# A stored instruction order, searched again: the query weights' second transpose goes behind the tile transposes

## Chip, cores and metric

The kernel runs on one core of a Trainium2 chip. The metric is the device time of one execution in microseconds, the median of several runs. The profile is of one more execution of the same program.

## What is computed

One transformer block on x, 2048 rows of 448, in bf16: attention with a feature map in place of the softmax over keys, then a gated feed-forward part, each with a residual and a normalisation without weights ahead of it.

```python
h  = x + A(layernorm(x));  h2 = h + B(layernorm(h))
# A: 16 heads of 28
phi(t) = concat(softmax(t @ w_phi), softmax(-t @ w_phi))
kv = phi(k)^T v;  z = sum_s phi(k)
A = (phi(q) kv / (phi(q) z + 1e-6)) @ wo
# B: 448 -> 1792 -> 448
B = (sigmoid(y @ w_gate) * (y @ w_up)) @ w_down
```

## The kernel before

The 2048 rows are 16 tiles of 128. `build` does not emit instructions; it declares 884 tasks in a graph: a name, an engine (or two to choose from), a few instructions, what it depends on, and the PSUM banks it may take. `_Graph.stored` (L134) then reads a table of numbers, `ORDER` (L40). Each number is 32 times the task's index, plus four times the choice of banks, plus the choice of engine. Each engine executes its tasks in the order of the table, strictly one after another; `emit` (L255) adds the semaphore waits. SyncE's queue (SP) issues nearly all DMAs, in that order too. `TURNS` (L90) adds waits that the data do not need: the first task of each entry also waits for the second, to keep GpSimd (POOL) and VectorE (DVE) apart. `_Graph.order` (L155), which once made such tables from assumed durations, is not used while `ORDER` is filled.

The tasks in this text, with the lines under which the profile shows them:

- Loads at L468: `x` t (from tile t on), `wk`, `wv`, `wq` (raw key, value and query weights), `wph`, `wom` (eight pieces of the output weights), later `wg`, `wu`, `wd`.
- Fold of the key weights with w_phi: `kT` (TensorE transpose, L547), `WkT` (copy, L432), `wM` 1 (L562), `W2` 1 (copy, L432) into `Wk2`. `warm`, `fill` (L539, L995) are matmuls on zeros that keep TensorE (PE) busy; `kv0` (L710) opens bank 4.
- Fold of the query weights: `wqT` 0 and 1, two DMA transposes of `wq_raw` into `WqT` (L508, on SP); `wM` 0 (L562) needs both; `W2` 0 copies into `Wq2`.
- Tiles of x: `bst`, `agg`, `ve`, `rstd` (statistics; L590 to L596), `xn` (normalise, L609 or L610), then `xP`, `xT` (TensorE and a copy, L620 and L432) for tiles 0 to 3, and a DMA transpose `xT` 4, 6, ... 14 for two tiles each (L628, on SP).
- Keys and values (L644): pairs of 14 matmuls in two tasks, `pa` t and `pb` t (Wk2 and Wv of tile t; `va` 0, `vb` 0: Wv of tiles 0 and 1; `pa` 0, `pb` 0: Wk2 of both). A second half waits for its own first half. Then `ekp`, `ekm` (exponentials, ScalarE), `v1` (copy), `ss`, `rs`, `phi` (L685, L689, L691) and `kv` (L703), which sums over all tiles in bank 4; `kvz` (L758) takes it out.
- Queries (L743): `qa`, `q`, then `eqp`, `eqm` (L753).
- Output of pairs of tiles: `num` (L779), `ocp` (copy to `opm`, L432), `rSm`, `rr`, `b`, `c`, `rd`, `o`, `od` (VectorE, L795 to L826), `oT` (DMA transpose, L828; for pair 0 `oP` on TensorE, L815), `wr`, `woa`, `wo_` (L848, L840), the second statistics, `ve2`, `rstd2`, `hn` (L884), `hT` (DMA transpose, L902; for pair 0 `hP`, L894).
- Feed-forward part in five chunks of 2, 4, 4, 4 and 2 tiles: `ga`, `gu` (L941), `sig` (L950), `hh` (L958), `dn` (L975), `fin` (L982), `st` (L985).

The order before around the change. SP: x 0, wk 1, wk 0, x 4, wph, x 6, wv 1, wv 0, wom 0, wq 3, wq 2, wq 1, wq 0, x 8, x 12, wqT 1, wqT 0, xT 4, xT 6, wom 5, wom 2, xT 8. TensorE: 11 fillers, kT and xP of tiles 0 and 1, wM 1, a filler, va 0 (between the wM 1), vb 0, xP of tiles 2 and 3, pa 0, pb 0, pa 3, pb 3, pa 2, pb 2, wM 0 (1, 3, 2), pa 5, pa 4, pb 5, pa 6, pb 4, pb 6, pa 7, wM 0 (0), kv 0, kv 1, pb 7, qa.

```python
load(("wq", i), wq_raw[:, i, :], ...)                     # L505
task(("wqT", h_), "sp", 1.28, lambda e, h_=h_: e.dma_start_transpose(
    out=WqT[:, 2 * h_:2 * h_ + 2]..., in_=wq_raw[:, 2 * h_:2 * h_ + 2]...),
    [("wq", 2 * h_), ("wq", 2 * h_ + 1)], lat=0.9, kind="tr", size=200.0, bias=1.0)
```

Of the kernel before, what the change touches and what calls it, by code (L numbers as in the profile page):

```python
# [29 lines left out]
FIRST = [(0, 0), (0, 1), (0, 2), (0, 3), (1, 0), (1, 2), (1, 3)]  # L30
SECOND = [(1, 0), (1, 1), (1, 2), (1, 3), (0, 0), (0, 1), (0, 3)]
NWARM = 1
NFILL = 12

O_FIRST = [(0, 0), (0, 1), (0, 2), (0, 3), (1, 0), (1, 1), (1, 2)]
O_SECOND = [(1, 0), (1, 1), (1, 2), (1, 3), (0, 0), (0, 1), (0, 2)]
# [1 line left out]


ORDER = """  # L40
# [46 lines left out]
"""  # L87


TURNS = [(('rstd', 4), ('xn', 3)), (('phi', 0), ('xn', 9)), (('phi', 4), ('xn', 12)), (('phi', 7), ('xn',  # L90
         15)), (('phi', 10), ('phi', 9)), (('phi', 14), ('phi', 13)), (('ve2', 2), ('hn', 3)), (('rstd2', 2),
         ('hn', 3)), (('ve2', 4), ('o', 5)), (('rstd2', 4), ('o', 5)), (('rstd2', 3), ('od', 5)), (('rstd2',
         5), ('od', 7))]


class _Task:
# [4 lines left out]
class _Graph:  # L101
# [12 lines left out]
    def task(self, name, eng, occ, fn, deps=(), lat=None, bias=0.0, banks=None, until=(), kind=None, size=0.0,  # L114
             after=None, rows=128, pace=0.0, behind=(), engs=None):
        assert name not in self.tasks, name
        t = _Task()
        t.engs = [eng] if engs is None else list(engs)
        eng = t.engs[0]
        t.name, t.eng, t.occ, t.fn, t.bias, t.kind, t.size = name, eng, occ, fn, bias, kind, size  # L120
        t.deps = [d for d in deps if d is not None] + ([after] if after is not None else [])
        t.after, t.rows, t.pace, t.behind = after, rows, pace, list(behind)
        t.lat = self.LAT[eng] if lat is None else lat
        t.banks, t.until, t.got = banks, list(until), None
        t.start = t.finish = None
        t.idx = len(self.tasks)
        t.need = list(t.deps)
        self.tasks[name] = t
        return t
# [125 lines left out]
    def emit(self, rings):  # L255
        nc = self.nc
        done = self.stored(ORDER) if ORDER.strip() else self.order()
        for name, first in TURNS:
            self.tasks[name].need.append(first)
# [69 lines left out]
def build(nc, A_x, A_wqkv, A_w_phi, A_wo, B_w_gate, B_w_up, B_w_down, out):  # L329
# [19 lines left out]
    with ExitStack() as es:  # L349
# [643 lines left out]

        for i in range(NFILL):
            task(("fill", i), "pe", 0.22, lambda e: e.matmul(  # L995
# [40 lines left out]
```

## Time and profile before

| what | value |
|---|---|
| median of 3 runs | 205.62 us (205.51 to 205.68) |
| the profiled execution | 205.42 us |
| its span in the profile | 203.7 us |
| granted TensorE clock | 0.999 |
| TensorE busy | 195.8 us, 96% |
| VectorE busy | 134.2 us, 66% |
| ScalarE (ACT) busy | 94.6 us, 46% |
| GpSimd busy | 32.8 us, 16% |

The span runs from the first to the last instruction of the profiled execution; what lies around it is 1.7 us. "PE" is TensorE's matmuls, "PEld" its weight loads, "SPq" the instructions with which SP issues DMAs. "Idle before" an instruction names what ended the wait. The chain that ended last is followed back from the last instruction. Both pieces of one pair of half-array matmuls run at once, so neighbouring rows overlap.

### The profile page before, as it was taken

Reading aid. Unit: us, or ns where it says so; the run is one execution under the profiler, and the core shown is the slowest. Engines: PE = TensorE matmul, PEld = TensorE weight load, DVE = VectorE, ACT = ScalarE, POOL = GpSimd, SP = SyncE. Lnnn points to the kernel's source line nnn. Section 1 sums busy time; section 2 is a strip of 40 time slices with the busy share of each in tenths; the row PEclk is TensorE's granted clock in tenths of the full one; section 3 lists DMA queues with packets and bytes.
Section 4 is the critical chain, followed back from the end, with each engine's and each line's share of the span. In section 5 each row is a group of like instructions: output and inputs, shape, how many; then the busy total and the mean of one; then the engine's idle time right before and its main releaser. Section 6 shows DMA issues by size and latency. Waiting matters only on the chain.

```text
span 203.7 us, 5394 instructions
## 1 busy us (share of the span) xinstructions
PE 195.8 (96%) x2276; PEld 109.5 (54%) x2276; DVE 134.2 (66%) x304; ACT 94.6 (46%) x169; POOL 32.8 (16%) x51
## 2 busy tenths in 40 slices
PE   7997999998889999999999999999999999999994
PEld 2543546555446985554445555454444555786553
DVE  2979989897999995789949846722455313541412
ACT  2699999999999553344031441202224400442000
POOL 5516936660000200003000100110000000000000
PEclk9999999999999999999999999999999999999999
DMA  5999696653045283501250020050020000200141
GB/s 144 313 271 149 173 194 159 187 198 93 3 103 145 80 93 79 140 0 43 51 116 3 0 53 3 5 121 3 0 74 3 2 3 0 69 3 0 34 158 59
DMA packets 35109, 16.94 MB, mean 83 GB/s; under 512 B 26828, under 2 KB 34060, under 8 KB 35084
## 3 DMA queue, kind: packets, MB, share of 16 engines
q1 hardware_dynamic: 34812, 16.36, 33.5%
q8 instruction: 18, 0.29, 0.6%
q10 hardware_dynamic: 272, 0.23, 0.3%
q14 instruction: 7, 0.06, 0.1%
HBM read 8.98 MB, written 1.84 MB: 53 GB/s over the span
## 4 chain that ended last, share of the span: by engine, by line
PE 86%; DMA 5%; DVE 3%; SPq 3%; issue 1%; ACT 0%; DVEq 0%
PE bank L941 42%; PE bank L975 21%; PE bank L644 8%; PE bank L743 5%; PE bank L840 5%; DMA WqT<-wq_raw 3%; SPq L468 3%; PE bank L703 2%; DMA wq_raw<-in_A_wqkv_dram 2%; PE bank L779 1%; SPq L508 1%; DVE o_pad L807 1%; DVE opm L432 1%; DVE st L865 1%; PE bank L562 1%
## 5 line engine op out<-in xcount | busy, mean ns | idle before, releaser
L941 PE MATMUL bank<-xnT,wu_sb 64*128 64x512 bf16 (+1 forms) x490 | 87.6, 333 | 0.0
L941 PE MATMUL bank<-xnT,wg_sb 64*128 64x512 bf16 (+1 forms) x490 | 87.5, 333 | 0.0
L950 ACT ACTIVATE sg_sb<-bank 128x512 f32<-128x512 f32 (+1 forms) x70 | 34.6, 511 | 81.4 <-PE bank L941 75.6
L958 DVE SCALAR_TENSOR_TENSOR hh<-sg_sb,bank 128x512 bf16<-128x512 f32 (+1 forms) x70 | 39.0, 575 | 30.3 <-ACT sg_sb L950 28.0
L941 PEld LDWEIGHTS bank<-xnT,wg_sb 64*128 64x128 bf16 x490 | 45.0, 94 | 20.8 <-issue 2.8
L941 PEld LDWEIGHTS bank<-xnT,wu_sb 64*128 64x128 bf16 x490 | 44.8, 94 | 13.9
L975 PE MATMUL bank<-wd_sb,hh 128*128 128x448 bf16 (+1 forms) x238 | 43.1, 342 | 0.0
L975 PEld LDWEIGHTS bank<-wd_sb,hh 128*128 128x128 bf16 x238 | 22.9, 98 | 20.1 <-DVE hh L958 0.4
L982 DVE SCALAR_TENSOR_TENSOR x_sb<-bank,x_sb 128x448 bf16<-128x448 f32 (+1 forms) x17 | 9.8, 594 | 24.6 <-PE bank L975 24.5
L644 PE MATMUL bank<-Wv,xnT 64*128 64x448 bf16 x112 | 21.9, 350 | 0.1
L644 PE MATMUL bank<-Wk,xnT 64*128 64x448 bf16 x112 | 21.7, 350 | 0.2
L691 POOL TENSOR_TENSOR phi<-ek,rsum 128x896 bf16<-128x896 bf16 x10 | 16.8, 1688 | 8.9 <-DVE xn_pad L610 4.7
L685 DVE TENSOR_REDUCE ssum<-ek 128x32 f32<-128x896 bf16 x16 | 16.6, 1069 | 0.8 <-ACT ek L664 0.7
L753 ACT ACTIVATE eq<-bank 128x1024 bf16<-128x1024 f32 x16 | 16.6, 1062 | 0.2
L880 POOL TENSOR_TENSOR rs<-rs,neghalf 128x2 f32<-128x2 f32 x8 | 5.6, 698 | 59.5 <-DVE rs L878 59.2
L743 PE MATMUL bank<-xnT,Wq 64*128 64x512 bf16 x112 | 14.3, 377 | 0.0
L840 PE MATMUL bank<-wo_sb,oT 64*128 64x448 bf16 x112 | 13.0, 350 | 0.6 <-DVE rs L878 0.6
L432 ACT CAST opm<-bank 128x960 bf16<-128x960 f32 x13 | 12.0, 972 | 1.4 <-PE bank L779 1.4
L644 PEld LDWEIGHTS bank<-Wk,xnT 64*128 64x128 bf16 x112 | 9.2, 94 | 5.9 <-PE bank L644 1.5
L644 PEld LDWEIGHTS bank<-Wv,xnT 64*128 64x128 bf16 x112 | 9.2, 94 | 5.0 <-ACT WkT L432 0.4
L870 DVE TENSOR_TENSOR x_sb<-bank,x_sb 128x896 bf16<-128x896 f32 x7 | 7.5, 1087 | 3.4 <-PE bank L840 3.4
L666 ACT ACTIVATE ek<-bank 128x448 bf16<-128x448 f32 x16 | 8.9, 563 | 0.9 <-PE bank L644 0.9
(92 smaller groups left out, 168.0 us busy)
## 6 DMA issues: line engine op xcount, KB each, us to landing
wu_sb<-in_B_w_up_dram SPq DMA_DIRECT2D x4, 448.0 KB, 4.1
wg_sb<-in_B_w_gate_dram SPq DMA_DIRECT2D x4, 448.0 KB, 3.9
out_dram<-x_sb SPq DMA_DIRECT2D x15, 112.0 KB, 1.8
wd_sb<-in_B_w_down_dram SPq DMA_DIRECT2D x7, 224.0 KB, 2.8
x_sb<-in_A_x_dram SPq DMA_DIRECT2D x2, 448.0 KB, 4.8
x_sb<-in_A_x_dram SPq DMA_DIRECT2D x3, 224.0 KB, 4.4
wq_raw<-in_A_wqkv_dram SPq DMA_DIRECT2D x4, 128.0 KB, 3.7
Wv<-in_A_wqkv_dram SPq DMA_DIRECT2D x2, 224.0 KB, 4.8
```

What stands on the lines that cost most here:

```text
L432: return e.copy(dst, src) if hasattr(e, "activation") else e.tensor_copy(dst, src)
L644: r = e.matmul(bank[bk][:, 0:D], lhsT=half(xnT, hi)[:, t, k, :], rhs=half(w, hi)[:, k, :], start=(i == 0), stop=(i == 6), tile_position=(6 ...
L685: task(("ss", t), "dve", dve(896), lambda e, s=s: e.tensor_reduce(ssum[:, s, :].rearrange("p (a h) -> p a h", h=2), ek[:, s].rearrange("p ...
L691: task(("phi", t), None, 1.68, lambda e, t=t, s=s: e.tensor_tensor(phi[:, t % NPHI, :, :, 0:DH, :].rearrange("p a g d h -> p (a g) d h"), ...
L743: r = e.matmul(bank[bb[j]], lhsT=half(Wq2, hi)[:, k, 2 * g:2 * g + 2].rearrange("p c d h -> p (c d h)"), rhs=half(xnT, hi)[:, 4 * c:4 * c ...
L753: task((key, gp, c), "act", act_p(1024), lambda e, gp=gp, c=c, sg=sg, nm=nm: e.activation(eq[c][:, sg, 2 * gp:2 * gp + 2, :], wide[got(nm) ...
L840: r = e.matmul(bank[bb[j]][:, 0:D], lhsT=half(oT, hi)[:, pr % NO, j, k, :], rhs=half(wo_sb, hi)[:, k, :], start=(i == 0 and not res), stop ...
L941: r = e.matmul(bank[b][:, 0:N], lhsT=half(w, hi)[:, k, fs], rhs=half(hnT, hi)[:, t0:t0 + n, k, :], start=(i == 0), stop=(i == 6), tile_pos ...
L950: task(("sig", f_, c), "act", act_p(N), lambda e, j=j, N=N, nm=nm: e.activation(sg_sb[:, j % NSG, 0:N], bank[got(nm)[0]][:, 0:N], ACT.Tanh ...
L958: task(("hh", f_, c), "dve", dve(N), lambda e, j=j, N=N, nm=nm, f_=f_, c=c: e.scalar_tensor_tensor(hhT[c % 2][:, f_, 0:N], sg_sb[:, j % NS ...
L975: r = e.matmul(bank[b][:, c0:c1], lhsT=hhT[c % 2][:, f_, o:o + P], rhs=wd_sb[:, f_, c0:c1], start=(f_ == 0), stop=(f_ == FT - 1))
L982: task(("fin",) + nm[1:], "dve", dve(c1 - c0), lambda e, nm=nm, tt=tt, pr=pr, c0=c0, c1=c1: e.scalar_tensor_tensor(X(tt)[:, c0:c1], bank[g ...
```

## The change

Four fillers more, a new table, and other turns. Nothing else in the code differs: the same tasks, dependencies and instructions.

```diff
-NFILL = 12
+NFILL = 16
 ORDER = """
-544 737 0 128 320 1152 448 609 352 27904 480 577 27936 512 768 160 9120 192 640 96 27968 224 288 28000 800 256
+544 737 0 320 1152 288 768 608 27904 224 480 577 27936 512 448 992 27968 128 256 160 28000 384 640 192 96
...
-TURNS = [(('rstd', 4), ('xn', 3)), (('phi', 0), ('xn', 9)), (('phi', 4), ('xn', 12)), (('phi', 7), ('xn',
-         15)), (('phi', 10), ('phi', 9)), (('phi', 14), ('phi', 13)), (('ve2', 2), ('hn', 3)), (('rstd2', 2),
-         ('hn', 3)), (('ve2', 4), ('o', 5)), (('rstd2', 4), ('o', 5)), (('rstd2', 3), ('od', 5)), (('rstd2',
-         5), ('od', 7))]
+TURNS = [(('rstd', 4), ('xn', 3)), (('phi', 2), ('xn', 8)), (('phi', 6), ('phi', 4)), (('phi', 14), ('phi',
+         13)), (('rstd2', 0), ('rr', 3)), (('ve2', 4), ('hn', 7)), (('rstd2', 4), ('hn', 7)), (('rstd2', 7),
+         ('hn', 12))]
```

Read out of the new table:

- SP: x 0, x 4, wk 0, wq 3, wph, x 6, x 8, wv 1, wv 0, wq 2, wq 1, wom 3, wom 1, x 12, wq 0, wqT 1, xT 4, xT 6, wom 0, wqT 0, xT 8. `wk` 1 is issued by ScalarE.
- TensorE: 12 fillers, kT and xP of tiles 0 and 1, wM 1 (1, 0), kv0, wM 1 (2), 3 fillers, wM 1 (3), xP of tiles 2 and 3, a filler, va 0, pa 2, pb 2, pa 0, vb 0, pb 0, pa 3, pb 3, pa 5, pa 4, pb 5, pa 6, pb 4, pb 6, kv 0 to 2, wM 0 (1, 3, 0), pa 7, wM 0 (2), pb 7, kv 3, pa 8, qa.
- Between 45 and 65 us: qa 3, num 0, 1, q, num 3, 2, 5, qa 2, num 7, q, num 6, 4, qa 2, q, oP, wr 0, woa 0, wo_ 0, qa 3, num 10, 9, q, woa 1, num 11, wo_ 1, hP, woa 2, num 13, wo_ 2, num 8, ga. (Before: num 0 to 2 in a row, num 3 to 6 in a row, both qa 2, num 7, oP, wr 0, woa 0, wo_ 0.)
- ScalarE takes `xn` 6, 7, 9, 10, 15 (7, 8, 11 before); VectorE takes `v1` 9, 10, 12 (13 before), one of the query folds' copies, `phi` 0, 1, 4, 7, 13, 15 (3, 5, 8, 9, 13, 15 before) and `ocp` 0, 3, 5, 9 (0, 3, 8 before).
- The feed-forward part has the same tasks in another order of the 14 column blocks within the chunks.

90 rows, old and new, of the table ORDER are left out of this document.

## The prediction

> **What bounds the kernel now.** I read the page first, then the chain that ended last, then TensorE's own instructions in order of time.
>
> ```profile
> span 203.7 us, 5394 instructions
> ...
> PE 195.8 (96%) x2276; PEld 109.5 (54%) x2276; DVE 134.2 (66%) x304; ACT 94.6 (46%) x169; POOL 32.8 (16%) x51
> ...
> PE   7997999998889999999999999999999999999994
> ...
> PE 86%; DMA 5%; DVE 3%; SPq 3%; issue 1%; ACT 0%; DVEq 0%
> ```
>
> TensorE (PE) is busy for 96% of the span and is 86% of the chain. So the time is TensorE's work, plus its holes, plus what lies before its first useful matmul. Only the first slices and those around 45 to 65 us are not full. The chain, and then TensorE's rows, say where the holes are:
>
> ```profile
> 12.00 6.05 DMA WqT<-wq_raw
> ...
> 18.10 0.77 PE bank L562 x12
> 18.86 4.85 PE bank L644 x50
> ...
> 26.18 0.37 PE bank L703 x16
> 26.54 0.76 PE bank L743 x6
> ...
> 35.79 0.65 PE bank L743 x6
> ...
> 44.89 1.64 PE bank L703 x96
> ```
>
> ```profile
> 6.50 1.01 PE L547 MATMUL bank<-ident,wk_raw 128*112 128x128 bf16 x8 [0.31 <-DMA wk_raw<-in_A_wqkv_dram]
> ...
> 9.66 0.93 PE L644 MATMUL bank<-Wv,xnT 64*128 64x448 bf16 x8
> ...
> 11.70 0.62 PE L620 MATMUL bank<-ident,xn_pad 128*128 128x128 bf16 x8
> 12.25 1.74 PE L644 MATMUL bank<-Wk,xnT 64*128 64x448 bf16 x14
> ...
> 14.39 0.35 PE L644 MATMUL bank<-Wv,xnT 64*128 64x448 bf16 x1
> ...
> 14.82 0.36 PE L644 MATMUL bank<-Wv,xnT 64*128 64x448 bf16 x1
> ...
> 18.10 0.77 PE L562 MATMUL bank<-Wp,WqT 112*128 112x112 bf16 x12 [0.97 <-DMA WqT<-wq_raw]
> ```
>
> ```profile
> 48.98 0.63 PE L779 MATMUL bank<-kvz,eq 64*128 64x60 bf16 x32 [0.15 <-DVE opm L432]
> 49.87 0.40 PE L779 MATMUL bank<-kvz,eq 64*128 64x60 bf16 x16 [0.26 <-ACT opm L432]
> 50.76 0.40 PE L779 MATMUL bank<-kvz,eq 64*128 64x60 bf16 x16 [0.49 <-DVE opm L432]
> ...
> 55.93 0.54 PE L848 MATMUL bank<-x_sb,ident 128*128 128x448 bf16 x2 [0.61 <-DVE oT L432]
> ...
> 60.74 0.93 PE L840 MATMUL bank<-wo_sb,oT 64*128 64x448 bf16 x8 [0.55 <-DVE rs L878]
> ```
>
> The bracket is TensorE's idle time and what ended it. At 18.10 it has waited 0.97 us for the second transpose of the query weights, `WqT`. That is the hole the change aims at. Five more, 2.06 us together, lie between 48.98 and 60.74: banks copied out too late, and the VectorE (DVE) chain of the first output pairs.
>
> **The change, part by part.**
>
> *The hole at 18.10.* In the new order the folds of the query weights stand behind `pb` of tile 6 and the first three `kv`. What removes the wait is that TensorE has `pa` 5, 4 and 6 to do first: **minus 0.97**.
>
> *The front of the queue.* On SP's queue `wk` 0 now goes behind x 4 (224 KB more in front of it), and `wv` behind `wq` 3 and x 8 (128 and 448 KB more).
>
> ```profile
> 4.12 0.98 SPq L468 DMA_DIRECT2D Wv<-in_A_wqkv_dram x2
> ```
>
> ```profile
> DMA to landing us min/median/max: 4.6/4.8/4.9
> ```
>
> ```profile
> 5.00:9.50 4.50, 4.19 (x38) 2.64 (x36) 4.47 (x17) 2.42 (x6) 2.99 (x6) 1.00 1.10 317
> 9.50:12.25 2.75, 2.67 (x31) 1.44 (x31) 1.35 (x9) 2.60 (x7) 1.01 (x1) 1.00 1.06 263
> ```
>
> The second row is that of the tile `Wv`; the last column of the windows is GB/s, the one before it the DMA engines' share, which is full. Today the second half of `Wv` lands at 4.61 + 4.9 = 9.5, and L644 starts at 9.66. With 590,000 bytes more ahead, at 263 to 317 GB/s, it lands 1.9 to 2.2 us later, at 11.4 to 11.7. `wk` 0 comes 0.7 us later (229,000 bytes at 317), so L547 starts near 7.2. The folds of the key weights hang on ScalarE (ACT), which is busy from then on:
>
> ```profile
> 8.93 0.99 ACT L432 COPY WkT<-bank 112x448 bf16<-112x448 bf16 x2
> ...
> 10.93 0.97 ACT L432 CAST Wk<-bank 128x448 bf16<-128x448 f32 x2 [0.15 <-PE bank L562]
> ```
>
> Its sixth copy ends at 9.92 and would end at 10.6; the last fold on TensorE, two tile transposes (0.55, from 11.70 to 12.25) and the last of the new fillers follow, so the first L644 starts at about **11.85**, later than `Wv` by little. The fillers lie in this wait and cost nothing; if `wv` came early they would cost 0.21 each. The last fold, 11.90 today, comes at 12.6, when `va` 0 ends. Today TensorE has finished the same tile transposes, and a whole pair of L644 as well, at 12.25. A pair is 14 matmuls at 4.85/50 = 0.097, so 1.36. Net: 1.36 - (12.25 - 11.85) = **plus 0.96**. The front gives back the whole hole.
>
> *Smaller terms of TensorE.* Where a pair's second half directly follows its first, the next matmul starts after 0.43 us (14.39 to 14.82), not 0.19: it waits for its own first half. Among the first four pairs this now happens twice, not three times: **minus 0.24**. A lone `kv` between 64-row matmuls takes 0.37 where six take 1.64 (0.25 each after the first), and the six matmuls of L743 behind it take 0.76, not 0.65: 0.23 for each such group. Between `pa` 5 and 45 us there are six groups, not seven: **minus 0.23**.
>
> *The transpose of tiles 4 and 5.* It moves ahead of `WqT` 0, into its place. TensorE reaches `pa` 5 at 11.85 + 4 x 1.36 + 2 x 0.24 = 17.8.
>
> ```profile
> 14.57 3.49 SPq L628 DMA_TRANSPOSE xnT<-xn_pad x2
> ```
>
> ```profile
> DMA to landing us min/median/max: 3.1/4.0/4.3
> ```
>
> ```profile
> q8 instruction: 18, 0.29, 0.6%
> ```
>
> ```profile
> q8 instruction: 1, 0.02, 2.2%
> ```
>
> ```profile
> 16.50:17.50 1.00, 0.62 (x6) 0.10 (x2) 1.00 (x2) 1.00 (x3) 1.00 (x2) 1.00 0.83 16
> ```
>
> The two queue rows are the page's, for the whole span, and the DMA view's of 15 to 18 us: one of 18 blocks of instructions is loaded there, and in 16.5 to 17.5 the wires carry 16 GB/s, with a transpose in flight. That is why I think the second `WqT` landed as late as 18.05. TensorE's 2276 matmuls and as many weight loads make 253 to a block, so I take the blocks for TensorE's, loaded as it goes on. With four more fillers its place in the useful work is 8 instructions sooner, and that work comes half a microsecond later, so I expect the block at the same moment, on the transpose of tiles 4 and 5. It would land at 18.05 too, **plus 0.3** of wait (0 if the block misses it). Above: issued when `wq` 2 has landed and the first `WqT` is out, near 13.5, plus 4.3 is 17.8; as late as today's (14.57 + 4.2) it is 18.8, a wait of 1.0.
>
> The Trainium skill, "Runtime: NRT & Kernel Launch", section "Instruction fetch mechanics", says that engines refill instructions in 16 KiB blocks over their own DMA queue, at a cost that is mostly hidden. The block's size agrees; that it is hidden does not, by the 16 GB/s above. By that rule the 0.3 falls away.
>
> *ScalarE, VectorE, GpSimd.* ScalarE gets two more normalisations, gives two `v1` and one fold to VectorE; VectorE's six `phi` are others (0, 1, 4, 7 for 3, 5, 8, 9). ScalarE's queue ends its last `eqm` of 47.7 at the same time, because it waits for TensorE there. GpSimd (POOL) is idle enough to hide `ve2`. I cost these at nothing; their cover is TensorE's backlog, and where it fails it is in the next term.
>
> *45 to 65 us.* The `num` are spread between L743, and `wr` takes other banks, which takes the 0.61 away; but `num` 9, `woa` 1 and `hP` wait for VectorE's chain:
>
> ```profile
> 61.64 0.73 DVE L884 TENSOR_SCALAR hn_pad<-x_sb,mv,rs 128x512 bf16<-128x512 bf16 x2
> ```
>
> That pair ends at 62.37 today. From `kvz` to it VectorE's queue now holds one more copy of `opm`, one product into `b_sb` and one copy into `x_sb` fewer, which is about even. So it moves with TensorE's lead at `kvz` (0.2 to 0.5), less what it waits for ScalarE's copies; I put it at 62.2. The stage hands on a lead of 0.2 to 0.4 and makes it no larger: **0**, bounded by plus 0.3 (lead lost) and minus 0.6 (the 0.61 gone).
>
> *The second chunk of L941.* It waits for the transposes of tiles 2 to 5.
>
> ```profile
> 72.23 0.73 DVE L884 TENSOR_SCALAR hn_pad<-x_sb,mv,rs 128x512 bf16<-128x512 bf16 x2
> ```
>
> ```profile
> 72.01 3.79 SPq L902 DMA_TRANSPOSE xnT<-hn_pad x2
> ```
>
> ```profile
> 77.61 0.37 PE L941 MATMUL bank<-xnT,wg_sb 64*128 64x512 bf16 x1
> ```
>
> ```profile
> DMA to landing us min/median/max: 2.7/2.8/4.8
> ```
>
> Today the normalised tiles are ready at 72.96, and TensorE stands from the end of L779 (16 matmuls from 77.16, 0.23 of work by the chain) to 77.61: 0.2. The way from the pair of tile 0 and 1 to there is 72.96 - 62.37 = 10.6; the new order puts a product into `b_sb` more on it, so I take 11.1: 73.3, and with 2.8 to land 76.1, before TensorE arrives at 77.2. **Minus 0.2**, between plus 0.8 (4.8 to land) and minus 0.2. From here on the windows would show TensorE full, as today, with the same work.
>
> Sum: -0.97 + 0.96 - 0.24 - 0.23 + 0.3 + 0 - 0.2 = **-0.4**, and I take **-0.45** for the fewer row switches left uncounted. The profiled execution took 205.42, 1.7 more than its span, and the median of the runs is 205.62; the sum gives 205.0 against the one and **205.15** against the other.
>
> **Rivals.**
> 1. *The block of instructions misses the tile transpose.* For it: it hit only some transposes today. Without the 0.3: 204.8. The rule of the Trainium skill named above would give this time.
> 2. *The lead is spent in the middle.* VectorE is busy without a hole from 49 to 60 us, and a lead that TensorE brings does not move it: only the 0.2 at 77.6 or nothing is left, 205.5.
> 3. *Slower: tiles 4 and 5 come late.* One mechanism: the in-order TensorE stands at `pa` 5 because its transpose, now third in line behind x 12 and the first `WqT`, lands at 18.8 or later. The price is 1 us for each microsecond past 17.8. It decides from 18.4 on, and everything on ScalarE and VectorE moves with it, so the later transposes wait too: 206.1. Against it: one transpose fewer ahead of it than today.
> 4. *The wait only moves.* `WqT` 0, issued near 17.6, may take the 5.2 to 6.1 us that the two took today:
>
> ```profile
> DMA to landing us min/median/max: 5.2/5.6/6.1
> ```
>
> It lands at 22.8 to 23.7; TensorE wants it near 22.9. Those took so long behind the loads of x, which are gone by then. If so, 205.8.
>
> **How the numbers follow.** Forecast 0.40 (205.15, of its own 204.8 to 205.5), rival 1 0.15, rival 2 0.15, rival 3 0.25, rival 4 0.05. A measurement of this kernel can tell about 0.2% from no change, 0.41 us: faster is below 205.2, slower above 206.0. Faster: half of the forecast's and all of rival 1's, with a little of rival 2, and stages in which more holes close than I count: 0.44. Slower: most of rival 3 and a part of rival 4: 0.26. Within: 0.30. The range runs from rival 1 with half of the 45 to 65 us bound (204.4) to rival 3 (206.3).
>
> **What would show it.** First L644 near 11.85 with a wait for `Wv` or ScalarE ahead of it; no wait for `WqT` at L562, and its first row near 23; a wait of 0.3 for `xnT` at about 18; at 45 us a lead of 0.5 on TensorE; 0.2 to 0.4 at the first L941; the second chunk at 77.2 without a wait. I am wrong if L644 starts after 12.4, if `pa` 5 waits a microsecond, or if TensorE shows holes after 65 us.

## The result

The changed kernel takes **206.62 us** (median of 10 runs, 206.25 to 208.68); the kernel before, run beside it, 205.15 (10 runs). The ratio is 1.0084, 95% interval 1.0061 to 1.0108: slower by 1.3 to 2.2 us, where 0.45 us faster was forecast. Two of the ten runs had a granted clock of 0.992 and took 208.28 and 208.68 us; without them the mean is 206.54, 1.3 us above the kernel before.

The page of the kernel after, the same lines as those of before:

```profile
span 205.0 us, 5405 instructions
...
PE 195.9 (96%) x2280; PEld 107.8 (53%) x2280; DVE 136.2 (66%) x303; ACT 94.2 (46%) x169; POOL 33.2 (16%) x52
...
PE   7899999998985999999999999999999999999994
...
PE 85%; ACT 7%; DMA 5%; DVE 1%; SPq 0%; issue 0%
```

The span grew by 1.3 us, TensorE's work did not. The 5 in TensorE's thirteenth slice (61.5 to 66.6 us) is new. TensorE's rows of that stretch, in order of time (all line numbers are one lower than before):

```profile
43.80 1.71 PE L702 MATMUL bank<-v,phi 128*64 128x58 bf16 x96
...
59.33 0.93 PE L839 MATMUL bank<-wo_sb,oT 64*128 64x448 bf16 x8 [0.62 <-DMA oT<-o_pad]
...
61.09 0.72 PE L893 MATMUL bank<-ident,hn_pad 128*128 128x128 bf16 x8
64.32 0.93 PE L839 MATMUL bank<-wo_sb,oT 64*128 64x448 bf16 x8 [2.52 <-DMA oT<-o_pad]
...
66.13 0.27 PE L940 MATMUL bank<-xnT,wu_sb 64*128 64x256 bf16 x1
```

The same places in the kernel before:

```profile
44.82 1.71 PE L703 MATMUL bank<-v,phi 128*64 128x58 bf16 x96
...
62.41 0.62 PE L894 MATMUL bank<-ident,hn_pad 128*128 128x128 bf16 x8
62.96 0.93 PE L840 MATMUL bank<-wo_sb,oT 64*128 64x448 bf16 x8
...
64.77 0.27 PE L941 MATMUL bank<-xnT,wu_sb 64*128 64x256 bf16 x1
```

At 43.80 us the new kernel leads by 1.0 us: the last large group of `kv` starts there, at 44.82 before. At 61.09 (`hP`) it still leads by 1.3. Then TensorE waits **2.52 us** for the transpose `oT` 2, which it did not before, and the feed-forward part starts at 66.13 instead of 64.77: 1.36 late. The span grew by 1.3, so that loss reaches the end. The chain after, and SP's queue after:

```profile
58.72 5.55 DMA oT<-o_pad
...
64.32 0.93 PE bank L839 x8
```

```profile
57.77 0.58 SPq L467 DMA_DIRECT2D wd_sb<-in_B_w_down_dram  x1
58.72 1.23 SPq L827 DMA_TRANSPOSE oT<-o_pad  x1
60.00 5.41 SPq L467 DMA_DIRECT2D wd_sb<-in_B_w_down_dram  x2
```

The transpose, which took 2.7 us from issue to landing before, took 5.55. It was not handed over late. VectorE's `od` 2, after and before:

```profile
58.50 0.20 DVE L825 COPY o_pad<-o_pad 128x128 bf16<-128x128 bf16 x1
```

```profile
58.61 0.19 DVE L826 COPY o_pad<-o_pad 128x128 bf16<-128x128 bf16 x1
```

What happened on the wires shows in the DMA view of 58 to 64 us: the GB/s of 40 slices of 0.15 us. First after, then before:

```profile
GB/s 288 285 295 272 64 0 48 137 131 143 269 358 287 156 168 213 256 273 191 106 2 0 0 0 0 0 0 0 0 0 7 9 9 9 12 65 294 303 384 370
```

```profile
GB/s 283 297 285 292 265 55 0 0 0 0 0 0 0 68 271 288 288 295 283 231 23 0 72 161 143 191 335 370 456 299 329 347 251 114 6 18 6 12 12 96
```

Before, `oT` 2 is the run between 59.95 and 61.15, at up to 295 GB/s and in one piece. After, it starts at 60.0, and from 61.0 to 63.25 the wires carry 0 to 12 GB/s; only then comes the rest. Meanwhile a block of instructions is loaded. The DMA view of 60.5 to 61.0 us (after) and of 62.0 to 62.5 (before):

```profile
q8 instruction: 1, 0.02, 23.3%
```

```profile
q8 instruction: 1, 0.02, 12.1%
```

The last column is a share of 16 engines in 0.5 us, so the block took 1.86 us after and 0.97 before. By the trace's DMA records it started at 60.69 and ended at 62.55; 19 packets of the transpose that had started by 61.0 all ended between 63.37 and 63.40. Before, the block came at 62.31, 0.8 us behind the landing of `oT` 2 (61.54).

### The profile page after: what moved, and what is told of

It reads as the page before. It is cut to its first block, busy times and chain, and to the rows that moved or that the text cites. A ratio compares the mean times of both kernels' runs of the same rounds, so it can differ in the third digit from the quotient of the medians.

```text
span 205.0 us, 5405 instructions
## 1 busy us (share of the span) xinstructions
PE 195.9 (96%) x2280; PEld 107.8 (53%) x2280; DVE 136.2 (66%) x303; ACT 94.2 (46%) x169; POOL 33.2 (16%) x52
## 4 chain that ended last, share of the span: by engine, by line
PE 85%; ACT 7%; DMA 5%; DVE 1%; SPq 0%; issue 0%
PE bank L940 42%; PE bank L974 21%; PE bank L643 11%; ACT eq L752 5%; PE bank L839 4%; DMA oT<-o_pad 3%; PE bank L742 3%; DMA wk_raw<-in_A_wqkv_dram 2%; ACT opm L431 2%; PE bank L702 1%; PE bank L561 1%; PE bank L546 1%; PE bank L778 1%; PE bank L619 1%; SPq L467 0%; PE bank L994 0%
## 5 line engine op out<-in xcount | busy, mean ns | idle before, releaser
L957 DVE SCALAR_TENSOR_TENSOR hh<-sg_sb,bank 128x512 bf16<-128x512 f32 (+1 forms) x70 | 39.5, 576 | 33.7 <-ACT sg_sb L949 33.0
L643 PE MATMUL bank<-Wk,xnT 64*128 64x448 bf16 x112 | 22.3, 350 | 0.1
L643 PE MATMUL bank<-Wv,xnT 64*128 64x448 bf16 x112 | 22.4, 350 | 0.0
L742 PE MATMUL bank<-xnT,Wq 64*128 64x512 bf16 x112 | 14.4, 377 | 0.6 <-DVE opm L431 0.5
L643 PEld LDWEIGHTS bank<-Wk,xnT 64*128 64x128 bf16 x112 | 8.9, 94 | 7.4 <-PE bank L643 1.0
L643 PEld LDWEIGHTS bank<-Wv,xnT 64*128 64x128 bf16 x112 | 8.8, 94 | 3.8 <-issue 0.3
L589 DVE BATCH_NORM_STATS2 st<-x_sb 128x6 f32<-128x448 bf16 x16 | 9.3, 604 | 0.7 <-DMA x_sb<-in_A_x_dram 0.7
```

Source lines behind the costliest of these rows:

```text
L643: r = e.matmul(bank[bk][:, 0:D], lhsT=half(xnT, hi)[:, t, k, :], rhs=half(w, hi)[:, k, :], start=(i == 0), stop=(i == 6), tile_position=(6 ...
L742: r = e.matmul(bank[bb[j]], lhsT=half(Wq2, hi)[:, k, 2 * g:2 * g + 2].rearrange("p c d h -> p (c d h)"), rhs=half(xnT, hi)[:, 4 * c:4 * c ...
L957: task(("hh", f_, c), "dve", dve(N), lambda e, j=j, N=N, nm=nm, f_=f_, c=c: e.scalar_tensor_tensor(hhT[c % 2][:, f_, 0:N], sg_sb[:, j % NS ...
```

## Experiments

**Theory A**: a block of TensorE's instructions stalls the DMA transpose that is in flight. The block hangs on TensorE's place in its program (its weight loads, matmuls and waits started before it were 1795 in the one kernel and 1804 in the other, which has four fillers more; in the runs below 1778 to 1811, and 1742 where the fillers are cut, while the time of the block goes from 58.78 to 63.70), the transpose on VectorE's chain. TensorE came 1.4 us sooner, VectorE 0.1, and so the two met. **Theory B**: the loads of `wd` beside `oT` 2 on SP's queue, which the new order put there, make it late. **Theory C**: VectorE does. Each ratio is to the kernel before on the same chip, with its 95% interval.

### The block moved ahead

```diff
     bs = got(("num", t))
-    for sg in range(2):
+    for sg in (0, 1) * (3 if t == 9 else 1):
```

> The changed kernel with the 16 matmuls of num 9 issued three times over (same inputs, same bank, same values): 64 more TensorE records (weight loads and matmuls) and 0.46 us, in a place where TensorE waits 0.62 us for the first transpose of oT anyway. Theory A (the block of TensorE instructions, which comes at a fixed count of its instructions, stalls the transpose of oT 2 in flight): the block that came at 60.69 comes between 58.4 and 59.4, oT 2 lands at 61.4 to 61.8 instead of 64.28, the hole of 2.52 us ahead of the third group of L839 shrinks to 0.3 or less, the first L940 comes near 63.8 instead of 66.13, and the time is 204.2 to 204.9 (206.62 less 1.7 to 2.4). Theory B (the loads of wd around oT 2 on SP's queue make it late): the hole stays, 206.6 to 207.1. Theory C (VectorE hands oT 2 over late): the hole stays, 206.6 to 207.1.

205.05 us, ratio 0.9986 (0.9956 to 1.0016). TensorE's row, and the wires from 58 to 64 us:

```profile
62.81 0.93 PE L839 MATMUL bank<-wo_sb,oT 64*128 64x448 bf16 x8 [0.66 <-DMA oT<-o_pad]
```

```profile
GB/s 184 282 294 290 288 292 113 111 30 102 66 143 287 341 293 182 114 201 266 204 127 29 16 19 111 278 294 259 162 119 179 305 341 215 108 18 0 0 0 0
```

More matmuls in a wait took the median from 206.62 to 205.05, 1.6 us: B and C fall as the whole cause. But 0.66 of the hole stays, twice what A expected. The block came at 59.16, with `wd` 2 in flight. One of the 16 parts of that load landed at 61.85, the first at 60.41 (DMA records), and the transpose behind it stood at 16 to 29 GB/s from 61.15 to 61.6. So it seems that a block that hits a load ahead of the transpose still stalls the transpose, by way of one late part.

### Half the dose

The same with `2 if t == 9`.

> The same with num 9 issued twice: 32 more records. Theory A: the block comes near 60.2, still with oT 2 in flight, but about half a microsecond sooner than in the changed kernel; oT 2 lands 1.7 us behind the block's end as there, at 63.3 to 63.9, the hole is 1.5 to 2.1 and the time 205.9 to 206.4. Theories B and C: hole 2.5, 206.6 to 206.9.

205.28 us, 0.9989 (0.9960 to 1.0017).

```profile
62.97 0.93 PE L839 MATMUL bank<-wo_sb,oT 64*128 64x448 bf16 x8 [0.46 <-DMA oT<-o_pad]
```

The block came at 59.52, not 60.2, again into `wd` 2. As a dose it failed: it is the first experiment once more, with the same outcome.

### The kernel before, block moved ahead

The edit of the first experiment in the kernel before, with `t == 8`.

> The kernel before with the 16 matmuls of num 8 issued three times over: 64 more records and 0.46 us of TensorE ahead of the wait of 0.55 us at 60.74. Theory A: the block that came at 62.31 comes between 60.1 and 60.8, with the transpose of oT 2 in flight, which lands at 62.9 to 64.0 instead of 61.54; a wait for oT 2 of 0.4 to 1.2 us appears ahead of the third group of L840 that was not there, and the time is 0.5 to 1.3 above the kernel before. Theories B and C: oT 2 lands at 61.5 as before, no wait for it; the time is 0 to 0.2 above the kernel before.

205.23 us, 0.9996 (0.9973 to 1.0018).

```profile
63.38 0.93 PE L840 MATMUL bank<-wo_sb,oT 64*128 64x448 bf16 x8
```

The block came at 61.29, when all but the tail of the transpose had run. 15 of the 16 parts of `oT` 2 landed between 61.70 and 61.78, the last at 63.34. That late landing is A's (62.9 to 64.0 expected, 61.5 under B and C). The cost that A expected is missing: TensorE arrived there at 63.3, when the transpose landed.

### The loads of `wd` held

The two loads cannot simply go behind `wd` 3, because `wd` 3 itself waits for `wd` 1; that form has no result. Here both wait for `oT` 2 instead.

```diff
-                 deps=([late[i - 2][0]] if i > 1 else []) + [
+                 deps=([late[i - 2][0]] if i > 1 else []) + ([("oT", 2)] if name in (("wd", 1), ("wd", 2)) else []) + [
 ORDER: 9472 (wd 2) goes behind 13056 (oT 2)
```

> The changed kernel with the loads of wd 2 and wd 1 held until oT 2 has landed, so that nothing but the transposes of oT is on SP's queue from 53 us on; TensorE's order is untouched. Theory A (the block of TensorE instructions stalls the transpose in flight): the block comes at 60.5 to 60.9 with oT 2 in flight, the wires stand still behind it until some 0.8 us past its end, oT 2 lands at 62.6 to 64.3, the hole is 0.9 to 2.6 and the time 205.2 to 206.7. Theory B (the loads of wd make oT 2 late): oT 2 lands at 61.4 to 61.7, the hole is below 0.3, the time 204.2 to 204.9.

205.76 us, 1.0035 (1.0018 to 1.0052).

```profile
63.79 0.93 PE L839 MATMUL bank<-wo_sb,oT 64*128 64x448 bf16 x8 [1.69 <-DMA oT<-o_pad]
```

```profile
GB/s 239 292 288 288 292 265 52 0 0 0 0 0 0 0 43 253 283 294 288 271 238 33 109 0 0 0 0 0 0 9 9 10 9 10 0 0 0 0 0 0
```

No load is near, and `oT` 2 still lands late, at 63.74. By the DMA records 997 of its 1024 packets of 256 bytes had started by 61.26; the block came at 61.45 and ended at 62.37, and the last 27 packets went one or two at a time from 62.35 on. That is A. The hole is 0.8 shorter than in the changed kernel, and the median 0.9 lower. In these two executions the length of the block covers that: 0.92 us here, 1.86 there. Whether the loads had a hand in it is asked below.

### Both

The loads held and `num` 9 three times over.

> The held loads of wd together with num 9 issued three times over, so that the block comes ahead of oT 2 and finds nothing in flight, not even a load whose tail the transpose would meet. Theory A: block at 58.9 to 59.4, oT 2 lands 2.7 us after its issue, at 61.3 to 62.0, hole below 0.4, time 204.2 to 204.9, faster than the kernel before (0.995 to 0.999). Theory B: as with the loads held alone. If the hole of 0.66 of the first experiment was not the tail of the load of wd 2, it stays and the time is 205.0.

204.59 us, **0.9974** (0.9956 to 0.9993).

```profile
61.77 0.93 PE L839 MATMUL bank<-wo_sb,oT 64*128 64x448 bf16 x8
```

```profile
GB/s 294 288 290 290 105 109 0 0 0 0 0 0 10 196 288 288 121 183 285 294 83 0 0 0 0 0 0 0 0 0 0 108 179 203 167 275 329 311 317 341
```

The block came at 58.84 and met nothing; `oT` 2 runs in one stretch and TensorE does not wait at 61.77. The kernel is faster than before, with 32 matmuls more than the changed one. Run again, with other runs of the kernel before beside it:

> The kernel with the held loads of wd and num 9 three times over again, beside the core alone on the same chip, for a second interval. Theory A: hole ahead of the third group of L839 below 0.4, 204.2 to 204.9, ratio 0.995 to 0.999.

204.32 us, **0.9961** (0.9945 to 0.9977), no wait either:

```profile
62.07 0.93 PE L839 MATMUL bank<-wo_sb,oT 64*128 64x448 bf16 x8
```

From a median of 206.62 to 204.59 and 204.32 is 2.0 to 2.3 us, most of the hole of 2.52.

### The transpose moved instead of the block

In the kernel before `oT` 2 is held until `num` 8 is done; in the changed one until `num` 11 is. Every engine's order stays (the table puts SP's tasks behind the one that is waited for).

```diff
-                    [("od", pr), opt(("wo_", pr - NO))], lat=0.9, kind="tr", size=200.0)
+                    ([("num", 8)] if pr == 2 else []) + [("od", pr), opt(("wo_", pr - NO))], lat=0.9, kind="tr", size=200.0)
```

> The kernel before with the transpose of oT 2 held until num 8 is done (60.21), and nothing else changed: the loads of wd stay behind it. Theory A: its packets run from 61.5 on, the block comes at 62.3 in the middle of them, oT 2 lands at 64.0 to 65.7 instead of 63.0, TensorE waits 1.0 to 2.7 us for it ahead of the third group of L840, and the time is 0.8 to 2.5 above the kernel before. Theory B or C: it lands 2.7 us after its issue, at 62.9 to 63.1, when TensorE arrives there (62.96), and the time is 0 to 0.2 above the kernel before.

206.67 us, 1.0081 (1.0050 to 1.0113).

```profile
63.86 0.93 PE L840 MATMUL bank<-wo_sb,oT 64*128 64x448 bf16 x8 [1.49 <-DMA oT<-o_pad]
```

```profile
GB/s 204 12 0 0 0 0 0 0 0 0 0 0 0 0 0 0 0 0 104 282 294 287 393 268 171 10 0 113 30 13 15 10 9 10 107 370 382 78 376 359
```

The kernel before, with its transpose slid under its own block (61.37 in this execution), loses as much as the changed kernel. `oT` 2 lands 4.3 us after its issue (59.55 to 63.82).

> The changed kernel with the transpose of oT 2 held until num 11 is done (61.09), 2.4 us later than today, and nothing else changed. Theory A: the block (60.7) is over when the packets start at 62.3, so the transpose takes 2.7 us and lands at 63.7 to 64.0, sooner than the 64.28 of the transpose issued 2.4 us earlier; hole 1.9 to 2.3, time 206.0 to 206.5. Theories B and C: it lands 5.5 us after its issue, at 66.5, or at the least later than in the changed kernel; the time is 208.5 or more, or above 206.7.

206.40 us, 1.0068 (1.0041 to 1.0095). SP's row and TensorE's:

```profile
61.15 1.38 SPq L827 DMA_TRANSPOSE oT<-o_pad  x1
```

```profile
63.92 0.93 PE L839 MATMUL bank<-wo_sb,oT 64*128 64x448 bf16 x8 [1.49 <-DMA oT<-o_pad]
```

Issued 2.4 us later than in the changed kernel, the transpose landed 0.4 us sooner (63.87 against 64.28). Here the block (61.05) was over when the packets started. Under C this could not be. B alone could have it, since `wd` 2 had landed at 61.08, before the packets started; against B stands the run with the loads held.

### The front of the kernel before

The hole of 0.97 us at 18.10 has the same sign: in the prediction's row the wires stand at 16 GB/s from 16.5 to 17.5, behind a block at 15.91. Can it be moved away without moving a load?

```diff
+        def filler(e, i):
+            n, w = (5, 102) if i < 5 else (4, 128)
+            for q in range(n):
+                r = e.matmul(bank[5][:, q * w:(q + 1) * w], lhsT=warm[:], rhs=warm[:, 0:w], start=True, stop=True)
+            return r
...
-                    for sg in range(2):
+                    for sg in (0, 1) * (3 if t == 9 else 1):
```

> The kernel before in its own order, with its 12 fillers cut into 53 shorter matmuls of the same time (82 more records ahead of 6.5 us) and num 9 issued three times over (64 more records and 0.46 us ahead of the wait of 0.55 us at 60.74). Theory A (the block stalls whatever transpose is in flight, and the hole of 0.97 us at 18.10, at which the change aimed, was such a stall too): the block of 15.91 comes at 11.5 to 12.5, ahead of the transposes; the second transpose of WqT lands at 16.3 to 16.9 instead of 18.05; TensorE does not wait at 18.10 (hole below 0.2); the block of 62.31 comes near 59.2, between the two transposes of oT, and oT 2 lands as before, near 61.5. Time 204.1 to 204.8, faster than the kernel before by 0.3 to 1.0 us with no load, transpose or fold moved. Theories B and C have nothing to say on WqT: the hole at 18.10 stays, and the time is that of the kernel before or up to 0.3 more.

205.69 us, 1.0018 (0.9993 to 1.0044): a miss.

```profile
17.51 0.76 PE L562 MATMUL bank<-Wp,WqT 112*128 112x112 bf16 x12 [0.72 <-DMA WqT<-wq_raw]
18.81 0.36 PE L644 MATMUL bank<-Wk,xnT 64*128 64x448 bf16 x1 [0.53 <-DMA xnT<-xn_pad]
```

The wires from 10 to 18 us, slices of 0.2:

```profile
GB/s 251 191 202 264 332 314 314 341 323 318 373 273 287 340 283 312 273 187 138 112 77 67 38 40 31 20 19 100 289 274 287 292 289 292 260 260 230 207 204 184
```

The block came at 12.09, ahead of the transposes as planned, but with the load of x 8 in flight, and x 12 followed. The wires sank to 19 to 40 GB/s from 14.4 to 15.4, and the transposes went on when x 12 had landed (15.70). It looks like the first experiment's remainder again: the stall moved, and the waits came to 1.25 us instead of 0.97. The later block came at 58.78 and met the tail of `oT` 1, which cost 0.35 us at 60.91.

### One load at a time

`wd` 2 moved behind `wd` 1, both following `oT` 2 at once:

> The changed kernel with wd 2 moved from ahead of oT 2 to behind wd 1 on SP's queue; the loads follow oT 2 at once. It asks what made the block's stall 2.5 us there and 1.7 with both loads held. If it is a load queued behind the transpose: hole 2.2 to 2.6, 206.3 to 206.8. If it is the load of wd 2 ahead, or only the moment at which the block comes: hole 1.4 to 1.9, 205.6 to 206.1.

206.10 us, 1.0047 (1.0014 to 1.0080).

```profile
63.09 0.93 PE L839 MATMUL bank<-wo_sb,oT 64*128 64x448 bf16 x8 [1.15 <-DMA oT<-o_pad]
```

`wd` 1 alone held until `oT` 2 has landed:

> The changed kernel with wd 1 alone held until oT 2 has landed; wd 2 stays ahead of it. If a load queued behind the transpose lengthens the stall: hole 1.4 to 1.9, 205.6 to 206.1. If it is the load of wd 2 ahead: hole 2.2 to 2.6, 206.3 to 206.8. If it is only the moment at which the block comes, it is what the kernel before this one gives.

206.55 us, 1.0081 (1.0053 to 1.0110).

```profile
64.32 0.93 PE L839 MATMUL bank<-wo_sb,oT 64*128 64x448 bf16 x8 [1.52 <-DMA oT<-o_pad]
```

By the medians, `wd` 2 ahead costs 0.4 to 0.9 us (206.62 and 206.55 with it, 206.10 and 205.76 without), though the intervals of the first two ratios and the third overlap. By the holes of single executions (2.52 and 1.52 with it, 1.15 and 1.69 without) it is not so plain; in the execution of 1.52 TensorE came to this place 1.0 us later than in the changed kernel's, 0.45 of it from the start, and `oT` 2 landed at 64.28 in both. Loads behind the transpose do not lengthen the stall (1.15 with two of them).

The DMA records say more of these single executions. Wherever the block hit `oT` 2 (the changed kernel, the two runs here, the run with the loads held, and the kernel before with `oT` 2 held), `oT` 2 landed 1.4 to 1.7 us behind the end of the block (1.1 in the late hit of the kernel before). So the length of the block goes into the hole, and the 1.86 us of the changed kernel's is the longest of the 252 blocks in the 14 profiles (median 0.99). The stall itself had two forms: with `wd` 2 ahead, 17 to 19 packets of the transpose stood until 63.4 and the rest behind them; without it, all but the last 27 to 29 packets ran on. What made that one block slow, and why `wd` 2 ahead changes the form, stays open.

### The core alone

In the kernel before: `wqT` 0 behind `xT` 6, the four query folds and their copies behind `pb` 7 and `v1` 6, all else as it was.

> The core of the change alone, in the kernel before: the second transpose of WqT behind those of tiles 4 to 7 on SP's queue, its four folds and their copies behind pb 7 (TensorE) and v1 6 (ScalarE), and nothing else moved. By the prediction's first step the hole at 18.10 goes (TensorE goes straight on to pa 5, lead 0.4 to 1.0 at pa 5). The folds find WqT landed (near 21). One bank serves two of them and their copies stand ahead of the first qa, which may cost 0 to 0.8 there. Theory A: what lead is left at wo_ 1 (0 to 1.0) brings the block of 62.31 to 61.3 to 62.3, past most of oT 2, so it costs 0 to 0.4; time 204.3 to 205.3. A rival (the lead is eaten by the first qa waiting for its folds): lead 0 or less at 27 us, 205.1 to 205.6.

206.91 us, 1.0080 (1.0062 to 1.0097): the rival, and worse.

```profile
24.60 0.80 PE L562 MATMUL bank<-Wp,WqT 112*128 112x112 bf16 x12 [0.56 <-ACT v L432]
26.46 1.04 PE L743 MATMUL bank<-xnT,Wq 64*128 64x512 bf16 x8 [1.06 <-ACT Wq L432]
```

The hole at 18.10 is gone, and 1.62 us of waiting for ScalarE's copies (one of `v`, one of a fold) takes its place. So the move placed like this is worth nothing; in the changed kernel the order around it gives TensorE other work while ScalarE copies.

## Why the prediction failed

**The step that failed** is the term for 45 to 65 us, put at 0 and bounded by plus 0.3 (lead lost) and minus 0.6. It measured +2.4: a lead of 1.0 at 43.80 us became 1.36 late at 66.13, by the wait of 2.52 for `oT` 2, under which a block of TensorE's instructions had come. The prediction had the pieces. It took a block to come at TensorE's count of instructions and to be able to stop a transpose, and its second rival had VectorE not follow TensorE's lead. It asked where the block would fall only at the transpose of tiles 4 and 5. Asked for every transpose on the path, the trace of before had the answer: `oT` 2 landed at 61.54, the block came at 62.31, a margin of 0.8 us, with TensorE to come sooner there by the 0.5 forecast and by part of the 0.55 that it waited at 60.74. It came 1.41 sooner (59.33). The Trainium skill ("Runtime: NRT & Kernel Launch", section "Instruction fetch mechanics") has the cost of a block mostly hidden; for TensorE's own instructions no row here speaks against it, but the transpose beside it paid 2.8 us.

**The hole at 18.10**: right, it went. TensorE's rows of the front, after:

```profile
6.53 1.01 PE L546 MATMUL bank<-ident,wk_raw 128*112 128x128 bf16 x8 [0.75 <-DMA wk_raw<-in_A_wqkv_dram]
...
11.20 0.93 PE L643 MATMUL bank<-Wv,xnT 64*128 64x448 bf16 x8
...
16.80 0.35 PE L643 MATMUL bank<-Wv,xnT 64*128 64x448 bf16 x1
17.08 0.36 PE L643 MATMUL bank<-Wk,xnT 64*128 64x448 bf16 x1
...
22.11 0.76 PE L561 MATMUL bank<-Wp,WqT 112*128 112x112 bf16 x12
```

But its 0.97 is one execution's. With the same front it was, in the kernel before with `num` 8 three times over and in the kernel before with `oT` 2 held:

```profile
18.32 0.77 PE L562 MATMUL bank<-Wp,WqT 112*128 112x112 bf16 x12 [1.07 <-DMA WqT<-wq_raw]
```

```profile
17.44 0.76 PE L562 MATMUL bank<-Wp,WqT 112*128 112x112 bf16 x12 [0.36 <-DMA WqT<-wq_raw]
```

**The front, plus 0.96, less 0.24 for a boundary**: mis-sized, the forecast was too slow there. `wk` 0 let TensorE start at 6.53 (6.50 before), not 7.2, with 224 KB more ahead of it; L643 started at 11.20, not 11.85. `pa` 5 starts at 17.08, where TensorE stood ready at 17.13 before: the front costs nothing. **Tiles 4 and 5, plus 0.3**: the block did come there (14.49), but the transpose landed at 17.03 and the matmul started 0.28 after its neighbour instead of 0.19: 0.1. Rival 3 did not happen. **`WqT` 0**: no wait at 22.11, so rival 4 did not either. **The groups of `kv`, minus 0.23**: not seen. At `pa` 5 the lead is 1.0 already (18.81 before against 17.08, less 0.71 for the folds that stood ahead of it before), and 1.0 still at 43.80. **Lead at 45 us**: 1.0, not 0.5.

**The 0.61 at `wr` 0** went as forecast; 0.62 for `oT` 1 came at 59.33. The hn pair ended at 61.35 (60.63 + 0.72 in the trace), not 62.2. **The second chunk, minus 0.2**: nothing; its first wide matmul starts 12.84 us behind the first of the feed-forward part in both (77.61 - 64.77, 78.97 - 66.13).

```profile
78.97 0.37 PE L940 MATMUL bank<-xnT,wg_sb 64*128 64x512 bf16 x1 [0.18 <-issue]
```

Without the meeting the rest of the change, with `wd` held and 32 matmuls more, is worth 0.3 to 0.4% (the two runs of the cleared kernel), 0.5 to 0.8 us. That this lies near the 0.45 of the forecast is luck: the front and the tiles cost less than forecast, the second chunk and the groups of `kv` gave less.

## What to carry to other kernels

The loads of instruction blocks are DMAs that nobody issues: here they moved with the place of the engine that uses them up, while the transposes hung on another engine's chain. A reorder that brings one engine forward can slide the one over the other, so compare every block with every transfer that something waits for, in the whole kernel, not only where the change is. A wait that grew without a late hand-over and without more bytes is to be looked for in the wires' GB/s in slices of some 0.15 us.

## What the hardware showed beside that

- A block of 16 KB delays the DMA transpose that it meets. In the 14 profiles, 16 transposes `oT` had a block start 0.8 to 2.25 us after their issue; they landed 3.65 to 5.55 us after it, and 1.0 to 1.9 us behind the end of the block. The 52 that met no block between issue and landing took 2.71 to 2.78 us.
- That one of the 16 engines loads the block and falls behind with its part fits the late part of `wd` 2 (61.85 against 60.41), that of `oT` 2 (63.34 against 61.70), and the last 27 packets of `oT` 2 in the run with the loads held, fewer than the 64 that are a sixteenth of its 1024. The records do not name the engine, so it is not shown.
- A load between the block and the transpose seems to pass the stall on (0.66 us in the first experiment, 0.72 and 0.53 in the front of the kernel before).
- The start varies. The same first matmul of `wk`, in two executions of the same front:

```profile
6.23 1.01 PE L546 MATMUL bank<-ident,wk_raw 128*112 128x128 bf16 x8 [0.72 <-DMA wk_raw<-in_A_wqkv_dram]
```

```profile
7.17 1.01 PE L546 MATMUL bank<-ident,wk_raw 128*112 128x128 bf16 x8 [1.85 <-DMA wk_raw<-in_A_wqkv_dram]
```

  That is 0.9 us, more than the change was forecast to bring: one execution's span is no measure of such a change. Its holes say where the time went, but they vary too (0.36 to 1.07 us for the one at 18.10).
